# Fused attention and Fourier mixing on one core: full-form score tiles leave the visits, and the first batch's tables, turns and norm are rearranged

## The chip, the cores and the metric

The kernel runs on one core of a Trainium2 chip. TensorE (PE in the views, its weight loads PEld) multiplies matrices into PSUM, VectorE (DVE), ScalarE (ACT) and GpSimd (POOL) do the rest, and SyncE (SP) and GpSimd issue transfers. The metric is the device time of one execution in microseconds, lower is better.

## What is computed

```
scores = q @ k.T / sqrt(64);  attn = max(scores, 0)**2 / 448;  a = attn @ v     # 8 batches, 12 heads, 448 x 64
x = a as (8, 448, 768)
u = x + real(fft2(x over rows and columns))
un = (u - mean(u)) / sqrt(var(u) + 1e-6)          # over the 768 columns
out = u + max(un @ w_ch1, 0) @ w_ch2              # 768 -> 3072 -> 768
```

The inputs and the output are float32 in memory. The matmuls take bf16 operands and sum in float32.

## The kernel before

**Tiling.** Scores are made transposed, keys on the partitions. A batch has 12 heads in three groups of four. A group's keys are cut into seven tiles for the score stage: tiles 0 to 2 and 4 to 6 belong to a pair of heads each, one head on partitions 0 to 63 and one on 64 to 127, and their two matmuls of 64 rows run side by side (array form 64*128 in the trace, *row form* below). Tile 3 holds the last 64 keys of two heads at a time, zero-padded to 128 rows, and its two matmuls use the whole array (128*128, *full form*; `r == 3` in `score`, L993 to L1004). ScalarE takes a tile from PSUM with a relu (L1017, `squares`), VectorE or ScalarE squares it (L1034 or L1031, `square`), and `value` (L865) multiplies it with v: the full-form tile in one matmul (L870), the others in pairs of 64 columns each (L875, 128*64, *column form*). Six such value sets make a batch's attention. Then `fold` scales it into xT (L721 and L719 for the first batch).

**Mixing.** The transforms are matmuls with cosine and sine tables: over the channels (`first_channels`, L1457, for the first batch; L1482 after), a copy to bf16 (`pc`, L1501), over the rows (L1079, L1294). A mean and variance by BN_STATS, a square root on ScalarE, a norm into un, and a turn of un by matmuls (`turn`, L1180) give unT, which the first projection (L1986) reads. The later batches are stored and turned by transfers.

**Tables.** `build_dft` forms angles in turns on VectorE (L372 to L376: multiply and round to an integer, subtract it, take the absolute value) and sines on ScalarE (L381). `seq_table` forms the row tables on GpSimd (L406 to L414), VectorE (L421 to L425) and ScalarE (L431). `root_table` loads the square-root functions on ScalarE (L448).

**What sets the order.** Every stage is a generator that asks for its next operation; `ORDER`, a string of codes (L74), says for each step which of the waiting generators goes on. `CHOICES` (L109) fixes their decisions by number. So the order of every engine is written out, and a kernel's own rules count only where neither string nor table decides. From the second batch on, attention runs in *visits* between the projection matmuls: `attention` (L882) puts out up to three score tiles and one value set in one step, `LEAD` (L2220) says how far ahead of the projections. Three PSUM buffers of two banks (psS, pool BS) hold score tiles, two single banks (psF, BF) values and projections. Until the first channel matmuls, `warming` (L2202) fills TensorE with matmuls whose result is not used (L2216); `turn` has some too (L1178, L1185).

**The first batch.** `load_group` (L504) issues loads on GpSimd; for its first group the indices of the tables and the identity follow the load of k. `turn_on_pe` (L654) turns q and k by transposes (L671) and a copy (L678). `first_tail` (L1057) runs rows, norm and turns of the first batch; the last 64 rows of its second tile, which belong to the second group of columns, are turned by a matmul of their own (`turn_rows`, L1255) and copied (L1260). In the prediction, the *first projection* is the first matmul of L1986.

## Time and profile before

| | |
|---|---|
| median of 3 timed runs | 564.68 us (564.63 to 565.0) |
| the profiled execution | 564.12 us |
| its span, first to last instruction | 562.1 us |
| TensorE's mean granted clock | 0.999 |
| moved by DMA | 82.46 MB, mean 147 GB/s |
| HBM | 62.91 MB read, 26.25 MB written |

The span leaves out what the execution does before the first and after the last instruction, some 2 us. A row of the timeline has the start in us from the span's start, the length in us, the engine, the line, the operation, output and inputs by name with their shapes, and a count of instructions; behind it in brackets the idle time before it and what ended that. Lengths of matmuls overlap, so their spacing is read from their starts. In the view of windows each pair is the busy time of an engine and its instructions.

### The profile page before, as it was taken

How to read it: one execution, taken by the hardware profiler on the slowest of the kernel's cores; microseconds unless marked ns; L12 is line 12 of the kernel's file. 1: busy time of each engine (PE TensorE's matmuls, PEld its weight loads, DVE VectorE, ACT ScalarE, POOL GpSimd, SP SyncE). 2: the span in 40 equal slices, each digit the busy share in tenths (PEclk: the TensorE clock that was granted, in tenths of full speed). 3: DMA queues.
4: the chain of work that ended last, by engine and by line, in shares of the span. 5: the costliest groups of instructions: out<-in, count | busy, mean ns of one | idle time of the engine just before them, and what ended most of it. 6: DMA issues, size and time to landing. Idle time of an engine off the chain costs nothing.

```text
span 562.1 us, 11345 instructions
## 1 busy us (share of the span) xinstructions
PE 555.1 (99%) x4306; PEld 363.7 (65%) x4306; DVE 427.1 (76%) x1035; ACT 330.2 (59%) x557; POOL 166.8 (30%) x255
## 2 busy tenths in 40 slices
...
GB/s 111 180 206 266 204 208 147 183 172 172 147 120 222 146 195 144 142 239 184 124 153 183 214 165 166 207 139 64 114 117 159 162 30 47 96 42 141 1 43 114
DMA packets 152692, 82.46 MB, mean 147 GB/s; under 512 B 118077, under 2 KB 147901, under 8 KB 152637
## 3 DMA queue, kind: packets, MB, share of 16 engines
...
q8 instruction: 34, 0.56, 0.4%
q14 instruction: 22, 0.17, 0.1%
HBM read 62.91 MB, written 26.25 MB: 159 GB/s over the span
## 4 chain that ended last, share of the span: by engine, by line
PE 95%; DVE 1%; DMA 1%; ACT 1%; issue 0%; POOL 0%; DVEq 0%; POOLq 0%
PE psF L1986 27%; PE psF L2126 22%; PE psS L1002 8%; PE psS L2126 7%; PE psS L1817 7%; PE psF L875 5%; PE psF L2015 4%; PE psS L1482 2%; PE psF L1817 2%; PE psF L2040 1%; PE psF L870 1%; DMA kn<-in_k_dram 1%; PE psS L875 1%; PE psF L671 1%; PE psS L1457 1%; PE psS L1290 1%
## 5 line engine op out<-in xcount | busy, mean ns | idle before, releaser
L1017 ACT ACTIVATE sq<-psS 128x896 bf16<-128x896 f32 x168 | 145.9, 918 | 39.5 <-PE psS L1002 39.2
L1986 PE MATMUL psF<-unT,w 128*128 128x256 bf16 (+1 forms) x1296 | 165.6, 285 | 0.0
L1986 PEld LDWEIGHTS <-w 128*128 128x128 bf16 x1296 | 124.9, 98 | 38.0 <-issue 5.8
L2126 PEld LDWEIGHTS <-hT 128*128 128x128 bf16 x720 | 69.8, 98 | 47.0 <-issue 2.1
L1034 DVE TENSOR_TENSOR sq<-sq 128x896 bf16<-128x896 bf16 x138 | 82.5, 620 | 10.5 <-ACT sq L1017 9.9
L1973 ACT ACTIVATE hT<-psF 128x512 bf16<-128x512 f32 (+3 forms) x132 | 63.6, 503 | 41.3 <-PE psF L1986 40.8
L2126 PE MATMUL psF<-w,hT 128*128 128x384 bf16 x336 | 59.4, 326 | 0.0
L1674 DVE TENSOR_TENSOR o<-psF,o 128x384 f32<-128x384 f32 x73 | 40.4, 553 | 22.2 <-PE psF L2126 16.7
L1002 PE MATMUL psS<-qkT 64*128 64x448 bf16 (+1 forms) x336 | 51.8, 355 | 1.0 <-DVE qkT L678 0.9
L1832 ACT COPY copies<-psS 128x256 f32<-128x256 f32 x51 | 17.7, 376 | 53.5 <-PE psS L1817 40.2
L1391 POOL DMA_INDIRECT ubot<-u,backs x15 | 16.0, 1064 | 75.9 <-DVE u L1327 46.7
L1002 PEld LDWEIGHTS <-qkT 64*128 64x128 bf16 (+1 forms) x336 | 12.9, 94 | 32.7 <-issue 26.9
L524 POOL DMA_DIRECT2D qn<-in_q_dram x21 | 15.4, 735 | 61.7 <-DVE qkr L631 47.2
L875 PE MATMUL psF<-sq,vn 128*64 128x448 bf16 x234 | 31.5, 363 | 0.0
L1817 PEld LDWEIGHTS <-w 128*128 128x128 bf16 x288 | 28.2, 98 | 4.4 <-issue 0.7
L1334 DVE BATCH_NORM_STATS2 stats<-u 112x6 f32<-112x384 f32 (+2 forms) x56 | 29.8, 550 | 1.5 <-POOL u L1325 1.3
L737 DVE TENSOR_SCALAR xT<-psF 128x224 bf16<-128x224 f32 x56 | 19.8, 386 | 14.4 <-PE psF L875 14.1
L1391 POOL DMA_INDIRECT nbot<-un,backs x12 | 14.3, 1190 | 52.9 <-ACT un L1353 51.7
L1353 ACT ACTIVATE un<-u,small 112x768 bf16<-112x768 f32 (+2 forms) x28 | 28.7, 1029 | 1.3 <-DVE small L1340 0.9
L524 POOL DMA_DIRECT2D kn<-in_k_dram x21 | 16.1, 768 | 44.8 <-DVE qkr L631 37.8
L499 POOL DMA_DIRECT2D kn<-in_k_dram x42 | 25.8, 623 | 9.8 <-PE psF L1986 7.9
L1031 ACT ACTIVATE sq<-sq 128x896 bf16<-128x896 bf16 x30 | 28.3, 950 | 0.4
...
## 6 DMA issues: line engine op xcount, KB each, us to landing
...
```

What stands on the lines that cost most here:

```text
L524: nc.gpsimd.dma_start(out=to, in_=src[b, hs, 0:rows].rearrange("h (p j) d -> p h (j d)", j=j))
L875: nc.tensor.matmul(av[h * Dh:(h + 1) * Dh, 0:S], lhsT=vn_home[:, at:at + Dh], rhs=sq[:, h, :], start=start, stop=stop, skip_group_check=True)
L1002: nc.tensor.matmul(sc[:, h, 0:S].rearrange("k (c q) -> k c q", c=4), lhsT=flat[ps, k0:k0 + KB], rhs=qT[ps, pair], start=True, stop=True)
L1017: nc.scalar.activation(r, sc[:, :, 0:S], AF.Relu)
L1034: nc.vector.tensor_tensor(r, r, r, op=ALU.mult)
L1334: nc.vector.bn_stats(stats[:n, hf, :], u[:n, hf * (D // 2):(hf + 1) * (D // 2)])
L1391: nc.gpsimd.indirect_dma_start(out=bot, out_offset=bass.IndirectOffsetOnAxis(ap=(back if b < PAR else back2)[ch][:n], axis=0), in_=get(us[ ...
L1674: nc.vector.tensor_tensor(o[:, cols], pc[:, cols], o[:, cols], op=ALU.add)
L1817: nc.tensor.matmul(ps[:, 0:N], lhsT=lhs, rhs=rhs[:, m], start=(start and m == 0), stop=(stop and m == 2), skip_group_check=True)
L1973: nc.scalar.activation(hs, ps, AF.Relu)
L1986: nc.tensor.matmul(ph[:, i * N:(i + 1) * N], lhsT=w1_sb[m][hf][:, (jj + i) * 128:(jj + i + 1) * 128], rhs=unT[:, m, 0:N], start=(m == 0), ...
L2126: nc.tensor.matmul(pc[:, cols], lhsT=lhs[i], rhs=rhs[i][:, cols], start=(start and i == 0), stop=(i == KP - 1), skip_group_check=True)
```

## The change

- **Visits** (`attention`): outside the early visits, a full-form tile that is next gets a step of its own with no values. Otherwise a visit takes the tiles up to the next full-form one, that is one set of three. Where the values use a score buffer because two chains of the second projection are open, the visit takes no scores instead of up to two. LEAD falls from 2.9 to 2.5.
- **Tables**: the absolute value is an AND on the bits. The row tables are formed on VectorE alone from the channel tables' column indices, right after those; GpSimd's four steps and a rounding step on VectorE go. The table of square roots no longer waits for a copy.
- **First loads and turns**: the indices come right after the load of q. The first group's k is turned in two parts: three quarters as soon as the main part of k is there, the last quarter (filled by two later loads) by four transposes and one copy.
- **First norm and turn**: the third tile's norm goes from one GpSimd operation to two halves on ScalarE. The second tile is turned by 127 columns at once, and the later 64 are copied from the same bank (`second_part`), which then is held until this copy; the extra six matmuls go.
- **Squares**: the first batch's last square is no longer tied to ScalarE.
- **Order**: ORDER and CHOICES are new. In the whole program ScalarE has 14 squares instead of 30, VectorE 154 instead of 138. VectorE also takes some more of the projection's relus.

Of the two tables one line each; the rest of the difference in full, without context:

```diff
-CODES = '0123456789ABCDEFGHIJKLMNOPQRSTUVWXYZ'
+CODES = '0123456789ABCDEFGHIJKLMNOPQRSTUVWXY'
...
-    '009000000200999999999999999991111N1N029919999909199G102NN10991F111888MM4400F11L88L88884L088M84L1',
+    '000900000200999919999919919991N1N999102199G19NN10029912G902NN299225522G1M99M99919005M199N95M1099',
...
-    78: 0, 80: 1, 94: True, 99: False, 177: False, 190: True, 209: True, 226: 2, 238: True,
+    94: True, 107: 1, 121: False, 142: 4, 152: 2, 191: False, 232: True, 239: True, 252: 0,
...
@@ -363,0 +365,2 @@
+    SEQ_AT, SEQ_RANK = 3, 0.3
@@ -376 +379,2 @@
-            nc.vector.scalar_tensor_tensor(g, f, -1.0, f, op0=ALU.mult, op1=ALU.max)
+            nc.vector.tensor_scalar(g.bitcast(mybir.dt.int32), f.bitcast(mybir.dt.int32), 0x7FFFFFFF, None,
+                                    op0=ALU.bitwise_and)
@@ -384,0 +389 @@
+        nc.vector.tensor_scalar(row[:, 0:2], row[:, 4:6], 1.0 / S, None, op0=ALU.mult)
@@ -398,0 +404,2 @@
+            if m == SEQ_AT:
+                yield from seq_table()
@@ -399,0 +407,2 @@
+        if SEQ_AT == 3:
+            yield from seq_table()
@@ -403,9 +412,3 @@
-        f = work.tile([128, 4 * KH], FP32, name="dfty", tag="uA", bufs=1)
-        g = work.tile([128, 4 * KH], FP32, name="dfty", tag="uB", bufs=1)
-        yield need("POOL", 0.55)
-        nc.gpsimd.iota(drow[:, 0:2], pattern=[[128, 2]], base=0, channel_multiplier=1,
-                       allow_small_or_imprecise_dtypes=True)
-        nc.gpsimd.iota(dcol[:, 0:SX], pattern=[[1, SX]], base=0, channel_multiplier=0,
-                       allow_small_or_imprecise_dtypes=True)
-        yield need("POOL", 0.3)
-        nc.gpsimd.tensor_scalar(drow[:, 0:2], drow[:, 0:2], 1.0 / S, None, op0=ALU.mult)
+        f, g = (work.tile([128, 4 * KH], FP32, name="dfty", tag=t, bufs=1)[:, 0:2 * SX] for t in ("uA", "uB"))
+        whole = g.bitcast(mybir.dt.int32)
+        cols = dcol2.rearrange("p (t k) -> p k t", t=2)[:, 0:SX // 2]
@@ -413,4 +416,9 @@
-            e = yield need("POOL", 0.45)
-            nc.gpsimd.tensor_scalar(f[:, i * SX:(i + 1) * SX], dcol[:, 0:SX], drow[:, i:i + 1], None, op0=ALU.mult)
-        f, g = f[:, 0:2 * SX], g[:, 0:2 * SX]
-        sch.add(seq_sines(f, g, e + LATENCY["POOL"]), (0, 0.3))
+            at = slice(i * SX, (i + 1) * SX)
+            fi, wi = (y[:, at].rearrange("p (k t) -> p k t", t=2) for y in (f, whole))
+            yield need("DVE", dve(SX))
+            nc.vector.tensor_scalar(wi, cols, drow[:, i:i + 1], None, op0=ALU.mult)
+            yield need("DVE", dve(SX))
+            nc.vector.scalar_tensor_tensor(fi, cols, drow[:, i:i + 1], wi, op0=ALU.mult, op1=ALU.subtract)
+        e = yield need("DVE", 0.4)
+        nc.vector.tensor_scalar(whole, f.bitcast(mybir.dt.int32), 0x7FFFFFFF, None, op0=ALU.bitwise_and)
+        sch.add(seq_sines(f, g, e), (0, SEQ_RANK))
@@ -420,7 +427,0 @@
-        e = yield need("DVE", 0.4, [e])
-        nc.vector.tensor_scalar(g.bitcast(mybir.dt.int32), f, 1.0, None, op0=ALU.mult)
-        yield need("DVE", 0.55)
-        nc.vector.tensor_tensor(f, f, g.bitcast(mybir.dt.int32), op=ALU.subtract)
-        e = yield need("DVE", 0.4)
-        nc.vector.tensor_scalar(g.bitcast(mybir.dt.int32), f.bitcast(mybir.dt.int32), 0x7FFFFFFF, None,
-                                op0=ALU.bitwise_and)
@@ -446,2 +447,2 @@
-        yield need("SP", 0.0, [dft_ready, last_relu, first_copied])
-        yield need("ACT", 1.5, [first_copied])
+        yield need("SP", 0.0, [dft_ready, last_relu])
+        yield need("ACT", 1.5, [dft_ready])
@@ -480 +481 @@
-    arrived = {}
+    arrived, main_keys, ends_turned = {}, Cell(), Cell()
@@ -484,0 +486,2 @@
+        if (i, x) == (0, 1) and len(arrived[i, x]) == 1:
+            main_keys.t = landed[-1]
@@ -528 +531 @@
-            if i == 0 and x == 1:
+            if i == 0 and x == 0:
@@ -531,0 +535 @@
+            if i == 0 and x == 1:
@@ -587 +590,0 @@
-        yield from seq_table()
@@ -660 +663,3 @@
-        turned[b][g] = (pairs[:, :, 4 * KB:].rearrange("q r (c p) -> q r c p", c=4), flat, (KB, 4 * (KB + R)))
+        first = i == 0
+        turned[b][g] = (pairs[:, :, 0:4 * R].rearrange("q r (c p) -> q r c p", c=4), flat[:, 4 * R:], (KB, 4 * (KB + R)))
+        w = 4 * R + (3 if first else 4) * KB
@@ -663 +668 @@
-                e1 = yield need("PE", 4 * 0.07, ready[i][x:x + 1], [] if x else [BF],
+                e1 = yield need("PE", 4 * 0.07, [main_keys] if first and x else ready[i][x:x + 1], [] if x else [BF],
@@ -668,2 +673,2 @@
-                n, at = ((R, 4 * KB), (KB, 0))[x]
-                for c in range(4):
+                n, at = ((R, 0), (KB, 4 * R))[x]
+                for c in range(3 if first and x else 4):
@@ -678 +683 @@
-            copy(pairs[:, r], pt[:, 0:4 * (KB + R)])
+            copy(pairs[:, r, 0:w], pt[:, 0:w])
@@ -680,0 +686,12 @@
+        if first:
+            e1 = yield need("PE", 4 * 0.07, ready[i][1:2], [BF])
+            ptf = BF.take()
+            pt = ptf.bitcast(BF16)[:, 0:2 * KB].rearrange("q (r p) -> q r p", r=2)
+            for r in range(2):
+                for h in range(2):
+                    nc.tensor.transpose(pt[h * Dh:(h + 1) * Dh, r], loads[i][1][:, 3, 2 * r + h, :], ident)
+            e2 = yield need("DVE", 0.28, [e1 + LATENCY["PE"]])
+            nc.vector.tensor_copy(pairs[:, :, w:], pt)
+            BF.give(ptf, e2)
+            ends_turned.t = e2 + LATENCY["DVE"]
@@ -863 +880,3 @@
-        return turned_at[b][g] if r == 3 else [turned_at[b][g][r > 3]]
+        if r == 3:
+            return turned_at[b][g] + [ends_turned] * (b == 0 and g == 0)
+        return [turned_at[b][g][r > 3]]
@@ -895 +914,13 @@
-            n = min(1 if few else 3, NB - p)
+            if not few and p < NB and p % 7 == 3 and left is None and p + 1 - past(pv) <= room:
+                lead = b + p / NB
+                lead -= LEAD - SLOPE * (B - lead)
+                own = lambda: progress[0] >= lead
+                e = yield need("PE", 2 * mm(S), turned_for(b, p), [BS], own)
+                sc = score(b, p)
+                p += 1
+                fresh.append(p)
+                sqs[p - 1] = [None, Cell(), None]
+                sch.add(squares(b, [(p - 1, sc, e)], sqs), (0.2, 0.2))
+                continue
+            n = min(1 if few else 3, NB - p, NB if few else (3 - p) % 7 or 7)
@@ -915 +946 @@
-                        homes, n = BS, min(n, 2)
+                        homes, n = BS, 0
@@ -1021 +1052 @@
-            sch.add(square(b, r, e + LATENCY["ACT"], sqs[i][1], b == 0 and i == NB - 1), (0.2, 0.2))
+            sch.add(square(b, r, e + LATENCY["ACT"], sqs[i][1]), (0.2, 0.2))
@@ -1028,2 +1059,2 @@
-    def square(b, r, t, done, scalar):
-        if scalar or b >= ELASTIC[0] and sooner(t, "ACT", act(2 * S), "DVE", dve2(2 * S)):
+    def square(b, r, t, done):
+        if b >= ELASTIC[0] and sooner(t, "ACT", act(2 * S), "DVE", dve2(2 * S)):
@@ -1171,0 +1203,2 @@
+            if t == 1:
+                idn, w = rev[:, 0:127], 127
@@ -1182,0 +1216,2 @@
+            if t == 1:
+                BUN[0].free.append(e)
@@ -1198 +1233,2 @@
-                BS.give(pts[t][0], last)
+                if t != 1:
+                    BS.give(pts[t][0], last)
@@ -1204,0 +1241,8 @@
+        def second_part():
+            e = yield need("DVE", dve(6 * 64), [done[1][0]])
+            nc.vector.tensor_copy(groups[1][2][:, :, 0:64].rearrange("p (h m) w -> p h m w", h=2),
+                                  pts[1][0][:, :, 0:384].rearrange("p h (m w) -> p h m w", w=128)[:, :, :, 63:127])
+            BS.give(pts[1][0], e)
+            second_un[0].t = e + LATENCY["DVE"]
@@ -1224 +1268,2 @@
-        yield from norm(2, 0, "POOL")
+        yield from norm(2, 0, "ACT")
+        yield from norm(2, 1, "ACT")
@@ -1244 +1289 @@
-        sch.add(turn_rows(uns[0][1], max(t_un[1]), 128, rev[:, 63:127], 0, 64, "DVE", second_un[0]), (1, 1))
+        sch.add(second_part(), (1, 1))
@@ -1257,2 +1301,0 @@
-        if done is second_un[0]:
-            BUN[0].free.append(e)
@@ -2220 +2263 @@
-    LEAD, MIXED, SPARE, ELASTIC = 2.9, 1, 0.5, (1, 99)
+    LEAD, MIXED, SPARE, ELASTIC = 2.5, 1, 0.5, (1, 99)
```

**Three places in the order.** Rows have the line, the operation, output and inputs, and the output's shape; line numbers are those of each kernel.

TensorE, second batch, in the early projections; psS_1169 and psS_1172 are row-form tiles (their second and both matmuls), psS_1175 is the full-form tile, qkT the turned q and k. Before:

```order
L1002 LDWEIGHTS qkT_919
L1002 MATMUL psS_1169<-qkT_919 128x448
L1002 LDWEIGHTS qkT_919
L1002 MATMUL psS_1172<-qkT_919 128x448
L1002 LDWEIGHTS qkT_919
L1002 MATMUL psS_1172<-qkT_919 128x448
L1002 LDWEIGHTS qkT_919
L1002 MATMUL psS_1175<-qkT_919 128x448
L1002 LDWEIGHTS qkT_919
L1002 MATMUL psS_1175<-qkT_919 128x448
L1986 LDWEIGHTS w1_0_0_432
L1986 MATMUL psF_1183<-unT_682,w1_0_0_432 128x384
```

After, where the full-form tile of the same group stands (psS_1144):

```order
L2029 LDWEIGHTS w1_5_0_516
L2029 MATMUL psF_1135<-unT_685,w1_5_0_516 128x384
L1033 LDWEIGHTS qkT_910
L1033 MATMUL psS_1144<-qkT_910 128x448
L1033 LDWEIGHTS qkT_910
L1033 MATMUL psS_1144<-qkT_910 128x448
L2029 LDWEIGHTS w1_0_0_444
L2029 MATMUL psF_1148<-unT_685,w1_0_0_444 128x384
```

The full-form tile has left the two row-form ones and stands alone between two groups of projection matmuls; the next three row-form tiles follow a value set further on.

ScalarE, first batch, from the last relus (sq<-psS) to the first row copies (u). Before:

```order
L1017 ACTIVATE sq<-psS 128x896 x2
L719 ACTIVATE xT_111<-psF 128x224 x2
L1031 ACTIVATE sq<-sq 128x896
L719 ACTIVATE xT_111<-psF 128x224 x2
L431 ACTIVATE seqm<-dfty,few 128x480 x2
L431 ACTIVATE nseq<-dfty,few 128x480
L1501 CAST pc<-psS 128x2x193 x2
L678 COPY qkT<-psF 128x960
L448 ACT_TABLE_LOAD
L448 ACTIVATE drow<-few 128x1
L1131 COPY u<-psS 128x384
L1115 ACTIVATE small<-small,few 128x1
```

After:

```order
L736 ACTIVATE xT_111<-psF 128x224 x2
L1048 ACTIVATE sq<-psS 128x896
L432 ACTIVATE seqm<-dfty,few 128x480 x2
L432 ACTIVATE nseq<-dfty,few 128x480
L736 ACTIVATE xT_111<-psF 128x224 x2
L449 ACT_TABLE_LOAD
L449 ACTIVATE drow<-few 128x1
L1544 CAST pc<-psS 128x2x193 x2
L683 COPY qkT<-psF 128x960
L1162 COPY u<-psS 128x384
L1146 ACTIVATE small<-small,few 128x1
```

The square (L1031) is gone, the sines (L431, now L432) stand ahead of the last copy into xT, and the table load ahead of the pc copies instead of among the row copies.

VectorE, from the end of the memsets to the first copies of turned q and k. Before:

```order
L385 TENSOR_SCALAR drow<-drow 128x3
L372 TENSOR_SCALAR dftr<-dcol_114,drow 128x386
L374 SCALAR_TENSOR_TENSOR dfty<-dcol_114,drow,dftr 128x386
L376 SCALAR_TENSOR_TENSOR dfty<-dfty 128x386
L372 TENSOR_SCALAR dftr<-dcol_114,drow 128x386
L374 SCALAR_TENSOR_TENSOR dfty<-dcol_114,drow,dftr 128x386
L376 SCALAR_TENSOR_TENSOR dfty<-dfty 128x386
L441 TENSOR_SCALAR channeg<-chan_117 128x386
L372 TENSOR_SCALAR dftr<-dcol_114,drow 128x386
L374 SCALAR_TENSOR_TENSOR early<-dcol_114,drow,dftr 128x386
L376 SCALAR_TENSOR_TENSOR early<-early 128x386
L441 TENSOR_SCALAR channeg<-chan_118 128x386
```

The next row there is the first copy (L678). After, from the third table on:

```order
L375 TENSOR_SCALAR dftr<-dcol_114,drow 128x386
L377 SCALAR_TENSOR_TENSOR early<-dcol_114,drow,dftr 128x386
L379 TENSOR_SCALAR early<-early 128x386
L683 COPY qkT<-psF 128x832
L442 TENSOR_SCALAR channeg<-chan_118 128x386
L683 COPY qkT<-psF 128x832
L695 COPY qkT<-psF 128x2x128
L442 TENSOR_SCALAR channeg<-chan_119 128x386
L419 TENSOR_SCALAR dfty<-dcol_114,drow 128x240
L421 SCALAR_TENSOR_TENSOR dfty<-dcol_114,drow,dfty 128x240
L1065 TENSOR_TENSOR sq<-sq 128x896
```

The first copy stands one negation earlier, the last operation of a table is a TENSOR_SCALAR, and the row tables (L419, L421) stand between the first squares.

60 lines of the change are left out of this document (30 added, 30 removed), and 37 rows, old and new, of the table CHOICES.

## The prediction

> **What bounds the kernel now.** I read the page first: busy shares and the chain of work that ended last.
>
> ```profile
> span 562.1 us, 11345 instructions
> PE 555.1 (99%) x4306; PEld 363.7 (65%) x4306; DVE 427.1 (76%) x1035; ACT 330.2 (59%) x557; POOL 166.8 (30%) x255
> PE 95%; DVE 1%; DMA 1%; ACT 1%; issue 0%; POOL 0%; DVEq 0%; POOLq 0%
> ```
>
> TensorE is busy for 99% of the span, and 95% of the chain is TensorE. After the start, then, the time is the number of matmuls times their spacing, plus what the spacing loses between matmuls of unlike shape. The order of the program shows 4306 matmuls before and 4302 after, so columns streamed hardly change. What can change is the lost spacing, the waits, and the start, where a busy TensorE proves little because the page counts warming matmuls (L2216) as work.
>
> The view of waits, TensorE alone, from 60 us to the end, has one row:
>
> ```profile
> PE psF L1817 <- DVE hT L1837: 0.3, 1, 0.3
> ```
>
> Nearly no wait is left to remove after 60 us. There are two places to look: the form changes inside a visit, and the first 48 us.
>
> **Term 1: form changes.** The timeline of TensorE around one visit; columns are start, length, line, operands, array form, count:
>
> ```profile
> 49.52 0.55 PE L1002 MATMUL psS<-qkT 128*128 128x448 bf16 x2
> 49.91 3.10 PE L1986 MATMUL psF<-unT,w 128*128 128x384 bf16 x18
> 52.85 0.35 PE L870 MATMUL psF<-sq,vn 128*128 128x448 bf16 x1
> 53.13 0.76 PE L875 MATMUL psF<-sq,vn 128*64 128x448 bf16 x6
> 53.82 0.74 PE L1002 MATMUL psS<-qkT 64*128 64x448 bf16 x6
> 54.49 2.12 PE L1986 MATMUL psF<-unT,w 128*128 128x384 bf16 x12
> ```
>
> Read starts, since lengths of matmuls overlap. Two full-form score matmuls take 49.52 to 49.91, 0.19 us each, and the projection matmuls follow without a gap. Eighteen of those take 2.94 us, 0.163 each, and the full-form value matmul at 52.85 follows without a gap too. From 52.85 to 54.49 the visit takes 1.64 us. Its columns are one full matmul (0.19) and six pairs that run side by side (6 x 0.19), 1.33 us, plus some 0.03 between the pairs of L875. The other 0.28 us go to three changes of form: full to 64 columns, to 64 rows, back to full. That is **0.094 us a change**; a full-form tile between projection matmuls changes nothing.
>
> I counted the visits from the first projection matmul on in both orders. Before: 40 visits with values and row-form scores (3 changes each), 14 with row-form scores alone (2), 2 with values alone (2). After: 32, 9 and 10, and 20 full-form tiles alone, 19 of them with no change. With single changes at joins the orders have 154 and 136 in the visits; the second group of transposes keeps its 4. So 18 fewer: 18 x 0.094 = **-1.7 us**. The gain is less than a set of three full visits would suggest, because eight more value visits now stand without scores and pay two changes each; that is in the count. All of it is on the path, since TensorE is the chain there. A lone tile waits for one score bank, where a set waited for up to three, and only projections queue behind it. The lead of 2.5 instead of 2.9 lets attention run later; that costs nothing unless TensorE comes to wait, and stands in the bounds of the waits.
>
> The Trainium skill, page "TensorE: Matmul & The Clock Gate", section "Single matmul latency", gives a warm matmul whose drain is not hidden a constant of 398 cycles at 2.4 GHz beside its columns; as an estimate from that page a form change would cost 0.166 us, eighteen 3.0 us, and the time would be 560.5. The rows above show little more than half of that, and the rows decide.
>
> **Term 2: the first 48 us.** Nothing below rests on TensorE's busy time. It follows the chain from the tables on VectorE through the ScalarE relus to the first projection matmul.
>
> ```profile
> 3.08 0.18 POOL L310 IOTA drow<- 128x3 f32 x1
> 3.30 0.59 DVE L385 TENSOR_SCALAR drow<-drow 128x3 f32<-128x3 f32 x1 [0.98 <-POOL drow L310]
> 4.00 0.44 DVE L372 TENSOR_SCALAR dftr<-dcol,drow 128x386 int32<-128x386 f32 x1
> 5.12 0.56 DVE L376 SCALAR_TENSOR_TENSOR dfty<-dfty 128x386 f32<-128x386 f32 x1
> 9.31 0.65 DVE L678 COPY qkT<-psF 128x960 bf16<-128x960 bf16 x1
> 30.30 0.41 DVE L425 TENSOR_SCALAR dfty<-dfty 128x480 int32<-128x480 int32 x1
> 2.18 0.82 POOL L524 DMA_DIRECT2D qk<-in_k_dram  x1
> 6.82 0.48 PE L671 MATMUL psF<-ident,qk 128*64 128x128 bf16 x7
> 10.43 15.93 ACT L1017 ACTIVATE sq<-psS 128x896 bf16<-128x896 f32 x19
> ```
>
> *To the first relu.* The iotas pass the load of k (0.82 us of GpSimd), so L385's place starts at about 2.48; one more tiny operation stands there (0.2, an estimate from the 0.18 of small ones here), and the first table starts at 3.4 instead of 4.00, -0.6. Each table ends in a tensor_scalar on integers instead of L376. L425 is the same operation on 480 elements in 0.41; for 386 I take 0.36, -0.2 on each of three tables. Its bounds are 0.2 (columns alone at L425's rate) and 0.56 (no gain). One negation instead of two ahead of the first copy, -0.17. The copy of 9.31 moves to about 7.9. The load of k starts some 0.6 us later; its transposes began at 6.82 with time to spare, and at worst start at 7.45, which puts the copy at 8.2. Then four extra transposes wait for that copy's bank, about 0.3. The first relu starts at about 9.25 instead of 10.43.
>
> *To the last value.* The relus are 15.93 / 19 = 0.84 apart, and with two pairs of copies between them the last one ends at 27.9. VectorE is slower than that:
>
> ```profile
> 15.55 0.69 DVE L721 TENSOR_SCALAR xT<-psF 128x224 bf16<-128x224 f32 x2
> 16.68 0.65 DVE L678 COPY qkT<-psF 128x960 bf16<-128x960 bf16 x1
> 23.93 3.48 DVE L1034 TENSOR_TENSOR sq<-sq 128x896 bf16<-128x896 bf16 x6
> 30.63 0.83 DVE L796 TENSOR_TENSOR fold<-xT 128x225 bf16<-128x225 bf16 x4
> 30.75 0.38 PE L875 MATMUL psF<-sq,vn 128*64 128x448 bf16 x2
> ```
>
> It has 21 squares at 0.57 (the last was ScalarE's), four copies at 0.57 and three pairs of L721 at 0.6 (from start to next start), eight folds at 0.2 and five new sequence-table operations. Those run on 240 strided elements, which no row shows; the nearest are L372 (0.44) and L374 (0.62) on 386. I take 0.35 and 0.45, with 0.41 for the last, 2.0 in all; the bounds are 1.2 and 2.5. Together 19.6 us from 9.5, so the last square ends at 29.1 and its values run at 29.15 instead of 30.75.
>
> *To the rows.*
>
> ```profile
> 31.18 0.61 ACT L719 ACTIVATE xT<-psF 128x224 bf16<-128x224 f32 x2 [1.38 <-PE psF L875]
> 31.67 1.28 ACT L431 ACTIVATE seqm<-dfty,few 128x480 bf16<-128x480 f32 x2
> 29.66 1.16 PE L1457 MATMUL psS<-chan,fold 128*128 128x386 bf16 x6
> 31.43 0.70 PE L2216 MATMUL psS<-warm 128*128 128x252 bf16 x5
> 31.97 0.25 PE L1457 MATMUL psS<-chan,fold 128*128 128x193 bf16 x1
> 34.06 0.39 PE L671 MATMUL psF<-ident,qn 112*64 112x112 bf16 x8
> 34.61 0.54 PE L1079 MATMUL psS<-pc,seqm 128*128 128x384 bf16 x2
> ```
>
> Before, 24 channel matmuls stood behind the warming ones, 0.087 us each (31.97 to 34.06). After, behind the last value pair (0.3) stand 2 wide ones (0.36), 12 narrow (1.04), 11 warming (1.19) and 8 narrow (0.70): 3.6 us, ending at 32.75, -1.3. The three sines (0.64 each) come ahead of the last copy and end at 29.8, the copy (0.61) at 30.4, the last fold at 30.9, the square-root table (1.28, row below, and 0.3 for its first use) at 32.0: all beside the warming matmuls, which set the time. Rows start at 33.3.
>
> *To the first projection.*
>
> ```profile
> 35.68 1.28 ACT L448 ACT_TABLE_LOAD   x1
> 37.69 0.49 PE L1079 MATMUL psS<-pc,seqm 128*128 128x384 bf16 x2 [0.25 <-ACT u L1131]
> 42.87 0.29 ACT L1115 ACTIVATE small<-small,few 112x1 f32<-112x1 f32 x1 [0.99 <-DVE small L1109]
> 43.75 0.67 ACT L1154 ACTIVATE un<-psF,small 112x384 bf16<-112x384 f32 x1
> 46.84 0.95 ACT L678 COPY qkT<-psF 128x960 bf16<-128x960 bf16 x1
> 47.91 1.14 PE L1986 MATMUL psF<-unT,w 128*128 128x384 bf16 x6
> ```
>
> The wait of 0.25 for a bank goes, because the table load no longer stands among the copies. Against that, the third norm moves from GpSimd (L1152) to ScalarE in two halves of 0.67, ahead of the last root. That root waits until about 43.25 on the old clock instead of 42.87, and behind it are the last scale, norm, turn and copies: **+0.4**. The six matmuls of the extra turn go, but the first projection waited for the copy at 46.84 and not for TensorE, so I count nothing. The sum is -1.3 - 0.25 + 0.4 = **-1.15 us**; the projection starts near 46.75.
>
> GpSimd loses 4 us of sequence table, yet its later weight loads wait for earlier ones to land, so the loads come no sooner:
>
> ```profile
> 35.88 0.54 POOL L563 DMA_DIRECT2D w<-in_moe_w_ch_dram  x1 [1.28 <-DMA kn<-in_k_dram]
> ```
>
> The first norm on GpSimd stands behind this load and one of v, ends near 38.2, and its turn needs it at 40.4.
>
> **The sum.** -1.7 - 1.15 = -2.85. The profiled execution took 564.12 us (span 562.1); 561.3 after the change. The median of the timed runs is 564.68, 0.56 above it; on that scale I predict **561.8 us**. Ends: the start between -0.5 (tables no faster, new operations at 2.5) and -2.2 (VectorE keeps pace with the relus, the norm costs nothing); waits after 48 us between -0.7 and +1.5, since the order behind the start is new throughout.
>
> **Rivals.**
> 1. *The start is given back to a load.* The chain shows the third group's k for the second batch:
>
> ```profile
> 49.49 7.46 DMA kn<-in_k_dram
> ```
>
> It released TensorE near 57 us. If it lands no earlier, a projection that starts 1.15 us earlier waits 1.15 us longer there: 564.7 - 1.7 = 563.0. Against it: the new GpSimd order issues this load ahead of an indirect store. Chance 0.17.
>
> 2. *VectorE becomes the bound (slower).* ScalarE squares fall from 30 to 14, so VectorE gains 16 x 0.62, about 10 us, and some relus.
>
> ```profile
> 250.00:300.00 50.00, 50.00 (x383) 31.65 (x382) 42.95 (x101) 33.51 (x48) 17.92 (x24) 1.00 0.95 158
> ```
>
> In this 50 us stretch (busy time: PE, PEld, DVE, ACT, POOL) VectorE has 42.95, 86%; the added work, spread over 350 us, makes it about 89%. A late square then holds a value visit. There are 42; 2.85 us are lost from 0.07 us at each, and 0.15 us at each gives 561.8 + 6.3 = 568.1. Against it: the waits row above, next to nothing at 86%. Chance 0.06 slower, and 0.08 that half of it cancels the gain (564.5).
>
> 3. *Form changes dearer than 0.094 in the visits that go.* With a drain as long as a whole full-form matmul, 0.19, eighteen are worth 3.4 us: 560.1. All three in the visit above speak against it; 0.03.
>
> 4. *Order and tables move work, but TensorE hides it anyway.* Then only TensorE's own 1.7 counts, and a start pinned by the loads gives 563, as in rival 1.
>
> My forecast keeps 0.66. Faster by more than 0.2% (below 563.55; about what a measurement of this kernel can tell from no change) holds the forecast, rivals 1 and 3 but for their edge: 0.81. Within: 0.12. Slower: 0.07. The range 560.2 to 564.0 takes both ends of the start and most of the waits; 0.1 lies above, 0.1 below.
>
> **What would show it.** First relu near 9.3, last value near 29.2, rows near 33.3, first projection near 46.8; TensorE from there to the end 1.7 us shorter; a lone full-form tile that costs 0.38 us and no gap. Wrong if ScalarE's root for the last tile starts more than 0.4 us late, if a wait for VectorE or for k appears on TensorE after 48 us, or if the eight value visits without scores show more than two changes each.

## The result, and the profile after

The change made the kernel slower: **571.3 us**, median of 4 runs (568.88 to 573.43), against 564.65 for the kernel before (564.24 to 565.0). The ratio is 1.0117 [1.0076, 1.0158]. Forecast were 561.8 us and faster. The ratios here and below compare fast runs alone; a run over 1.5% above the fastest of its kernel (one of a1, one of after_again) is left out of them, though it stands in the medians and ranges. The profiled execution took 571.37 us, 7.25 more than the one of before. The page after, in its head, its busy shares and the engines' shares of the chain:

```profile
span 569.6 us, 11349 instructions
PE 554.6 (97%) x4302; PEld 365.1 (64%) x4302; DVE 442.1 (78%) x1062; ACT 315.7 (55%) x536; POOL 165.2 (29%) x249
PE 86%; DMA 8%; DVE 2%; POOL 2%; ACT 1%; issue 1%; DVEq 0%; POOLq 0%
```

The chain of before was 95% TensorE with 1% of DMA. Now 8% is DMA: somewhere the kernel waits for a transfer. The waits of TensorE: three rows of the start (to 50 us), then all rows from 50 to 115 us, and all from there to the end; behind the colon stand the sum, the count and the longest:

```profile
PE psF L676 <- DMA qk<-in_k_dram: 1.2, 1, 1.2
PE psF L693 <- DMA qk<-in_k_dram: 0.7, 1, 0.7
PE psS L1213 <- ACT unT L1231: 0.6, 1, 0.6
...
PE psF L2058 <- DMA w<-in_moe_w_ch_dram: 2.7, 1, 2.7
PE psS L1033 <- DMA qkT<-qkr: 1.5, 1, 1.5
PE psF L889 <- DMA vn<-in_v_dram: 1.0, 1, 1.0
...
PE psF L889 <- DVE o L1717: 1.1, 1, 1.1
PE psS L1033 <- ACT sq L1048: 0.4, 1, 0.4
PE psS L1033 <- ACT xT L751: 0.2, 1, 0.2
```

The same view of before had one row after 60 us, 0.3 us. The largest wait now is for a piece of the second projection's weights. The chain around it, in order of time (start, length, what):

```profile
59.92 34.21 DMA w<-in_moe_w_ch_dram
94.13 0.04 issue
94.17 3.54 PE psF L2058 x12
```

The piece, issued before 59.92, lands at 94.13. TensorE's timeline ahead of that, after and then before:

```profile
91.06 0.41 PE L1525 MATMUL psS<-chan,diff 128*97 128x193 bf16 x3
94.17 3.54 PE L2058 MATMUL psF<-w,hT 128*128 128x384 bf16 x12 [2.70 <-DMA w<-in_moe_w_ch_dram]
```

```profile
89.07 0.41 PE L1482 MATMUL psS<-chan,diff 128*97 128x193 bf16 x3
89.32 2.11 PE L2015 MATMUL psF<-w,hT 128*128 128x384 bf16 x12
```

Two things are to be seen. The matmuls start 2.86 us late (91.30, where the matmuls ahead have streamed, to 94.17), and the same twelve take 3.54 us instead of 2.11. The windows view tells why; its last three columns are the granted clock, the DMA share and GB/s:

```profile
91.00:94.00 3.00, 0.47 (x6) 0.33 (x5) 0.00 (x0) 1.53 (x2) 0.00 (x0) 0.95 1.50 160
94.00:98.00 4.00, 3.83 (x15) 1.92 (x15) 0.89 (x2) 0.00 (x0) 2.53 (x4) 0.61 1.53 160
98.00:102.00 4.00, 4.00 (x27) 2.52 (x25) 2.40 (x6) 0.99 (x2) 4.00 (x7) 1.00 1.34 159
```

After the idle stretch TensorE ran about 3 us at half clock (0.61 over the 4 us), which costs some 1.4 us more. The profiled execution's time then splits by starts on TensorE:

| | before | after | difference |
|---|---|---|---|
| first projection matmul starts | 47.91 | 49.01 | +1.10 |
| single waits over 0.15 us behind it, slowed matmuls included | 1.14 | 9.23 | +8.09 |
| the rest, up to the last matmul | 509.45 | 507.71 | -1.74 |
| last matmul starts | 558.49 | 565.94 | +7.45 |

A wait here is what a spacing of two matmuls has beyond the columns of the first, and beyond 0.1 us where the array form changes. So TensorE's own work shrank as forecast, and waits ate that gain more than four times over. The spread of this kernel's runs goes in part with the slowed stretch: those above 571 us have a mean clock of 0.994 to 0.997, the one at 568.88 has 1.000.

### The profile page after: what moved, and what is told of

Its sections match the earlier page's. It is cut to its first block, busy times and chain, and to the rows that moved or that the text cites. A ratio compares the mean times of both kernels' runs of the same rounds, so it can differ in the third digit from the quotient of the medians.

```text
span 569.6 us, 11349 instructions
## 1 busy us (share of the span) xinstructions
PE 554.6 (97%) x4302; PEld 365.1 (64%) x4302; DVE 442.1 (78%) x1062; ACT 315.7 (55%) x536; POOL 165.2 (29%) x249
## 4 chain that ended last, share of the span: by engine, by line
PE 86%; DMA 8%; DVE 2%; POOL 2%; ACT 1%; issue 1%; DVEq 0%; POOLq 0%
PE psF L2029 24%; PE psF L2169 23%; PE psS L1860 8%; PE psS L1033 7%; DMA w<-in_moe_w_ch_dram 6%; PE psS L2169 5%; PE psF L894 4%; PE psF L2058 2%; PE psF L1860 2%; PE psS L1525 2%; DMA qkT<-qkr 2%; PE psF L2083 1%; PE psS L894 1%; PE psF L889 1%; PE psF L676 1%; DMA qk<-in_k_dram 1%
## 5 line engine op out<-in xcount | busy, mean ns | idle before, releaser
L1065 DVE TENSOR_TENSOR sq<-sq 128x896 bf16<-128x896 bf16 x154 | 91.9, 619 | 13.5 <-ACT sq L1048 12.9
L2016 ACT ACTIVATE hT<-psF 128x512 bf16<-128x512 f32 (+2 forms) x123 | 60.1, 506 | 35.4 <-PE psF L2029 33.8
L2169 PE MATMUL psF<-w,hT 128*128 128x384 bf16 x378 | 67.4, 326 | 0.0
L1717 DVE TENSOR_TENSOR o<-psF,o 128x384 f32<-128x384 f32 x78 | 43.0, 552 | 27.6 <-PE psF L2169 16.4
L1875 ACT COPY copies<-psS 128x256 f32<-128x256 f32 x57 | 20.0, 376 | 41.7 <-PE psS L1860 36.7
L1434 POOL DMA_INDIRECT ubot<-u,backs x15 | 18.5, 1236 | 59.2 <-DVE u L1370 50.4
L1434 POOL DMA_INDIRECT nbot<-un,backs x12 | 13.0, 1084 | 71.5 <-ACT un L1396 50.8
L1033 PEld LDWEIGHTS <-qkT 64*128 64x128 bf16 (+1 forms) x336 | 15.3, 94 | 26.1 <-issue 17.8
L754 DVE TENSOR_SCALAR xT<-psF 128x224 bf16<-128x224 f32 x60 | 21.2, 384 | 12.9 <-PE psF L894 12.6
L894 PE MATMUL psF<-sq,vn 128*64 128x448 bf16 x228 | 30.2, 362 | 0.0
L2058 PE MATMUL psF<-w,hT 128*128 128x384 bf16 x144 | 26.3, 338 | 2.7 <-DMA w<-in_moe_w_ch_dram 2.7
```

Source lines behind the costliest of these rows:

```text
L894: nc.tensor.matmul(av[h * Dh:(h + 1) * Dh, 0:S], lhsT=vn_home[:, at:at + Dh], rhs=sq[:, h, :], start=start, stop=stop, skip_group_check=True)
L1033: nc.tensor.matmul(sc[:, h, 0:S].rearrange("k (c q) -> k c q", c=4), lhsT=flat[ps, k0:k0 + KB], rhs=qT[ps, pair], start=True, stop=True)
L1065: nc.vector.tensor_tensor(r, r, r, op=ALU.mult)
L1434: nc.gpsimd.indirect_dma_start(out=bot, out_offset=bass.IndirectOffsetOnAxis(ap=(back if b < PAR else back2)[ch][:n], axis=0), in_=get(us[ ...
L1717: nc.vector.tensor_tensor(o[:, cols], pc[:, cols], o[:, cols], op=ALU.add)
L2016: nc.scalar.activation(hs, ps, AF.Relu)
```

## The experiments

Theory W: the weights are the cause. GpSimd issues them later, so the last piece of w2 lands after it is read, and a long wait also costs clock. Theory S: the start is the cause, above all the load of k behind the iotas. Each set of runs shared its runs of the kernel before (medians 564.40, 564.40, 564.45 and 564.50).

Why the weights are issued later stands in GpSimd's timeline, before and after:

```profile
19.22 0.19 POOL L341 TENSOR_TENSOR backv<-backv 128x1 f32<-128x1 f32 x1
20.05 0.42 POOL L348 TENSOR_SCALAR_AFFINE_SELECT order<-order 128x57 bf16<-128x57 bf16 x2
20.64 3.37 POOL L563 DMA_DIRECT2D w<-in_moe_w_ch_dram  x6
```

```profile
19.87 0.56 POOL L342 TENSOR_TENSOR backv<-backv 128x1 f32<-128x1 f32 x1
21.34 0.80 POOL L349 TENSOR_SCALAR_AFFINE_SELECT order<-order 128x57 bf16<-128x57 bf16 x2
22.66 3.32 POOL L567 DMA_DIRECT2D w<-in_moe_w_ch_dram  x6
```

The first weights leave at 22.66 instead of 20.64. The small index instructions ahead of them (`mirrors`) begin 0.53 us later and take 4.24 us instead of 2.75, though none of them changed: four of them take about two to three times as long (0.56 for 0.19 us, 0.46 for 0.18, 0.80 for 0.42, 0.60 for 0.24), the index tables and memsets no longer than before. Beside them VectorE runs two-input squares and copies without a pause. It isn't the change alone that does this: in the second run of the same kernel (after_again) three of the four took 0.20, 0.43 and 0.24 us and the weights left at 21.74, and in a run of before with a longer `mirrors` (b_late) the four took 0.41 to 1.31 us.

### Set 1: three edits of after, and all of them

**a1_tables**: `mirrors` moves behind the issue of the first six weight pieces.

```
-            if i == NG + 1 and x == 1 and 0 in parts:
-                yield need("POOL", 3.6)
-                mirrors()
...
         yield from load_w1(0)
+        yield need("POOL", 3.6)
+        mirrors()
```

> The changed kernel with one thing moved: GpSimd's twelve small table instructions (rev, backs, order) run behind the issues of the first six weight loads and not ahead of them. Nothing moves on the other engines. Theory W (the weights land late, and TensorE waits for what queues behind them): the first weight piece is issued near 18.5 us instead of 22.66 and lands near 25.4 instead of 27.33; the last piece of the second projection's weights lands near 92 instead of 94.13; the waits at 80.4 (1.1 us, a load of v) and at 91.2 (2.9 us) shrink to under 0.2 and under 1, with them the 1.4 us of slow matmuls behind the second; time 566 to 568 us. Rival V (the searched order asks too early, DMA order means little): the waits move by under 0.5 us in all and the time stays at 570 to 571.5. Rival S (the loss is made at the start, before the first projection): also 570 to 571.5, as the start is untouched.

Measured: 564.96 us (563.57 to 572.86, 10 runs), 1.0016 [0.9991, 1.0041]. The weights leave at 18.75, the last piece lands at 90.04, the wait for it is 0.9 us at a full clock, and the wait for v is gone. This one edit, which changes no computation, takes back nearly the whole loss, more than theory W forecast, though two of its ten runs still took over 570 us.

**a2_iota**: the iotas go back behind the first load of k (in `load_group`).

```
-            if i == 0 and x == 0:
+            if i == 0 and x == 1:
                 e = yield need("POOL", 0.55)
                 dft_indices()
```

> The changed kernel with one thing undone: the two index tables (iota) of GpSimd stand behind the issue of the first load of k again, as before the change, not ahead of it. Both theories: the main part of k lands near 6.3 us instead of 7.29, the first projection starts 1 to 1.6 us earlier than 49.01. Theory W: weights come only 0.5 us earlier, so TensorE reaches them 0.5 to 1 us sooner than they do and gives the gain back at the waits of 80 to 110 us: time 570.3 to 571.3. Rival S (what is gained at the start stays gained): 569.5 to 570.

Measured: 565.6 us (564.98 to 566.72, 7 runs), 1.0026 [1.0015, 1.0038]. Both theories missed: the last load of k lands at 7.51 as before, but the first relu starts at 10.25, since the copies behind the tables on VectorE are now late (a wait of 1.2), and the first projection starts only 0.3 us earlier. The gain stands at the weights instead: GpSimd reaches them at 21.16, the last piece lands at 90.97, and the wait is 1.2.

**a3_vfirst**: the loads of v of the third group go ahead of the first two pieces of w2.

```
         yield from load_group(NG + 2, (0, 1))
+        yield from load_group(NG + 2, (2,))
         yield from load_w2(range(2))
-        yield from load_group(NG + 2, (2,))
```

> The changed kernel with one thing moved: the three loads of v for the third group of the second batch are issued ahead of the first two 1.1 MB pieces of the second projection's weights, not behind them. Theory W, with contention: these loads have fallen together with a DMA transpose and two reloads of rows (they took 5.6 us of the queue from 76.06 to 81.61, before the change 1.6); ahead of the weights they take under 2 us, so the last weight piece lands near 90.5 us instead of 94.13, the waits at 80.4 and 91.2 us fall from 4.0 to under 1 and the slow matmuls go; time 566 to 568. If the 4 us of the queue are owed to the transposes whatever lies in it, the last piece lands after 93 and the time is 569.5 to 571 (only the wait at 80.4 goes). Rival V: 570 to 571.5.

Measured: 565.95 us (564.37 to 570.62, 10 runs), 1.0041 [1.0013, 1.0068]. The last piece still lands late (91.38, a wait of 1.2).

**a4_all**: all three edits.

> The three edits together (tables behind the first six weight loads, index tables behind the load of k, the three loads of v ahead of the second weights). Theory W: last weight piece near 88 us, no wait over 0.5 us for a load between 50 and 100 us, start 1 to 1.6 us earlier; what is left over the kernel before are the waits of 190 to 201 us (2.2) and some of the 1.6 us at 107: time 562.5 to 565. Rival V: at least 568, since the order asks too early whatever the loads do. Rival S: 569.5 to 570, the gain of the index tables alone.

Measured: 565.77 us (563.95 to 566.62, 7 runs), 1.0017 [1.0004, 1.003]. The last piece lands at 89.21 and nothing waits for it. In its place TensorE waits 1.3 us for transposed q and k (`qkT<-qkr`) at 103 us. It is no better than a1 alone, and above theory W's 562.5 to 565: a removed wait came back behind another transfer. Of theory S the table above leaves 1.10 us of the 7.45, the later first projection.

### Set 2: the same again, and other places

**after_again**: the changed kernel, unedited, for its spread.

> The changed kernel as it is, a second time, beside the others of this set: how far its time and the landing of its loads spread from run to run. The wait for the last weight piece was 2.9 us in the first profile, and the three edits of the set before, each of which brings that piece forward by some microseconds, gave 565.0, 565.6 and 566.0 with runs up to 572.9. Theory W (TensorE asks for the piece at about the moment it lands, so the time hangs on the transfers): median 569 to 572, the lowest and highest run over 3 us apart, the kernel before within 1 us. Against it: a spread as small as that of the kernel before.

Measured: 569.07 us (565.79 to 574.48, 7 runs), 1.0092 [1.0058, 1.0125]. The profiled run took 565.96: the last piece of w2 lands at 91.57, the wait is 1.1 and the clock stays full. The same instructions with the same order thus land this piece at 91.57 in one run and at 94.13 in another; the first weights left at 21.74 there and at 22.66 here. The spread over 3 us is what theory W forecast.

**b_late**: before, with the first pair of instructions of `mirrors` run ten times, to make its weights late.

```
+        for _ in range(10):
-        nc.gpsimd.memset(rev, 0.0)
+            nc.gpsimd.memset(rev, 0.0)
...
```

> The kernel before the change with one addition: two of GpSimd's table instructions (rev) run ten times and not once, so that the first weight load is issued about 5.7 us later; nothing else moves, and the searched order is that of before. Theory W: in the kernel before the last weight piece lands at 86.33 us and is read at 89.32, 3.0 us of slack; with the loads 5.7 us later it lands near 92, TensorE waits 2 to 3 us there and some of the matmuls behind run at half clock as in the changed kernel: 568 to 571 us. If the loss of the changed kernel comes from its order and not from late weights, the time stays within 1.5 us of 564.4.

Measured: 573.2 us (571.67 to 573.56, 4 runs), 1.0146 [1.0131, 1.0161]. It misses its aim: the sequence table behind it on GpSimd came late too, and the waits stand elsewhere.

```profile
PE psS L1458 <- DVE fold L797: 3.2, 1, 3.2
PE psF L871 <- DMA vn<-in_v_dram: 2.8, 1, 2.8
```

TensorE reaches the last piece of w2 only behind its landing at 93.79. The run says nothing on W. It says something on the clock: behind the wait of 2.8 us (at 61 us) the trace has 3.4 us at half clock, behind the longer one of 3.2 us (at 36 us) none.

**c1_sp**: after, with the reloads of rows ahead of the transposes of xn on SP. The end of that stretch in the order of SP:

```
-L861 DMA_TRANSPOSE xn<-xT_110 128x4x128
 L1688 DMA o<-utop_72 96x384
 L1688 DMA o<-ulow 32x384
-L861 DMA_TRANSPOSE xn<-xT_111 128x4x128
 L1688 DMA o<-ulow 65x384
 L1688 DMA o<-ubot_80 63x384
-L861 DMA_TRANSPOSE xn<-xT_111 128x4x128 x2
+L861 DMA_TRANSPOSE xn<-xT_110 128x4x128 x3
+L861 DMA_TRANSPOSE xn<-xT_111 128x4x128 x3
```

> The changed kernel with SyncE's queue alone changed: seven reloads of rows (four of them of 192 KB), which stand behind DMA transposes that wait for the values of the second batch, are issued ahead of the first of these transposes, as before the change. Before, 928 KB went over the other queue while the second weights were loaded (57.3 to 86.3 us), after, 1501 KB (58.5 to 94.1). Theory R (the reloads slow the weights because they fall into their time): the stretch from the first to the last of these weights shortens by 2 to 4 us, the last piece lands at 90 to 92 instead of 94.13, time 566 to 569. Rival (the 16 engines move the same bytes in any order, so a reload that goes earlier only pushes the weights back): the last piece lands within 1 us of where it did, 570 to 572.

Measured: 568.51 us (567.48 to 571.01, 4 runs), 1.0066 [1.0051, 1.008]. In the profiled run, the slowest, the last piece lands at 93.84, the wait is 3.1 and the half clock follows. The landing is the rival's, within 0.3 us of where it was, and the median is within 0.6 us of after_again.

**c2_dve**: a1, with VectorE's two additions into u ahead of three copies and relus, at one place only. It goes at the wait for `o` (1.1 us, third part of the waits). The stretch of after, VectorE and then GpSimd beside it:

```profile
187.50 0.55 DVE L1368 TENSOR_TENSOR u<-qs,xn 112x385 f32<-112x385 f32 x1
187.97 2.62 DVE L1370 TENSOR_TENSOR u<-tp,xn 112x383 f32<-112x383 f32 x1
190.52 0.54 DVE L1717 TENSOR_TENSOR o<-psF,o 128x384 f32<-128x384 f32 x1
...
188.45 0.93 POOL L1368 TENSOR_TENSOR u<-tp,xn 112x385 f32<-112x385 f32 x1
189.32 0.85 POOL L1370 TENSOR_TENSOR u<-qs,xn 112x383 f32<-112x383 f32 x1
```

The second addition takes 2.62 us where its neighbour takes 0.55, while GpSimd adds two operands too; `o` behind it, and so a bank of TensorE, is late. The edit, in the order of VectorE:

```
-L2144 TENSOR_TENSOR hT<-hT 128x256
-L633 COPY qkr<-qn 112x1024
-L2146 TENSOR_TENSOR hT<-hT 128x256
 L1367 TENSOR_TENSOR u<-qs,xn 112x385
 L1369 TENSOR_TENSOR u<-tp,xn 112x383
+L2144 TENSOR_TENSOR hT<-hT 128x256
+L633 COPY qkr<-qn 112x1024
+L2146 TENSOR_TENSOR hT<-hT 128x256
```

> The kernel a1_tables with one step of VectorE moved: its two additions for rows of the first-mix output (u), which ran beside GpSimd's two additions of the same kind, go ahead of two small additions and one copy (qkr), so that they are done before GpSimd begins. In the changed kernel, and in the three edits of the first set, the second of these additions took 2.63 us and not 0.55, and TensorE waited 1.26 us for the addition behind it and 0.9 us 10 us later. Theory P (the two engines shut each other out while both add): that instruction takes 0.6 us again, the waits at 183.7 and 194 us shrink by 1 to 2.2 us in sum: 563 to 564.2 us. Rival (VectorE is simply behind its work there, wherever the two additions stand): within 0.5 us of a1_tables, 564.5 to 565.5.

Measured: 563.45 us (562.58 to 570.06, 12 runs), 1.0003 [0.9978, 1.0027]. In its trace the additions stand clear of GpSimd's, which begin at 182.72:

```profile
180.10 0.55 DVE L1367 TENSOR_TENSOR u<-qs,xn 112x385 f32<-112x385 f32 x1
180.57 0.55 DVE L1369 TENSOR_TENSOR u<-tp,xn 112x383 f32<-112x383 f32 x1
```

The wait is gone. The time against before stays within the interval, so what shows this part is the trace. The collision itself has moved: at 183.41 another two-input instruction of VectorE (`hT`, 0.28 us elsewhere) takes 1.20 beside GpSimd's second addition, and TensorE doesn't wait for it. The Trainium skill, page "SBUF — State Buffer", section "Who interferes with whom", states that a VectorE instruction with two inputs in SBUF contends with a GpSimd instruction that reads SBUF, that the shared ports are an exclusive lock, and that the order of issue decides who blocks. The 2.62 against 0.55 agrees with the contention; VectorE's addition is stamped 0.48 us ahead of GpSimd's and was held all the same.

### Set 3: the deadline itself

**d2_more**: before, with three more loads of 384 KB ahead of w2, which the program throws away (the last piece is loaded again in its turn). This makes the weights late in an order that is otherwise that of before.

```
+            if i == 0:
+                w2_sb[3] = wpool.tile([128, 6, D], BF16, name="w2_3")
+                for j in range(3):
+                    nc.gpsimd.dma_start(
+                        out=w2_sb[3][:, 2 * j:2 * j + 2],
+                        in_=moe_w_ch2[2304 + j * 256:2560 + j * 256, :].rearrange("(j p) d -> p j d", p=128))
...
```

> The kernel before the change with one addition: ahead of the first piece of the second projection's weights, three loads of 384 KB are issued that write the last piece's data a first time (the last piece is loaded again in its turn, so the output is the same). Every other instruction and the order of all engines are those of before. By the pace of its loads (1.9 to 2.4 us for 384 KB) all that queues behind lands about 6 us later: the third group's v near 80 us instead of 74.05 (read at 79.02), the last weight piece near 92.5 instead of 86.33 (read at 89.32). Theory W: waits of about 1 us near 79 and 2 us near 90, matmuls at half clock behind them in some runs, a later third group: 568 to 570.5 us with a spread of over 2 us. Rival (late weights cost this order nothing, the loss of the changed kernel sits in its searched order): 564 to 565.5 and the small spread of before.

Measured: 569.49 us (567.86 to 571.32, 4 runs), 1.009 [1.0071, 1.011]. The last piece lands at 93.22 and the picture of after appears, wait and clock; waits from 60 us on, timeline, and windows:

```profile
PE psF L2021 <- DMA w<-in_moe_w_ch_dram: 2.9, 1, 2.9
PE psF L1823 <- DVE hT L1843: 0.3, 1, 0.3
```

```profile
93.27 3.29 PE L2021 MATMUL psF<-w,hT 128*128 128x384 bf16 x12 [2.93 <-DMA w<-in_moe_w_ch_dram]
```

```profile
94.00:98.00 4.00, 4.00 (x16) 2.10 (x15) 0.89 (x2) 0.26 (x1) 1.57 (x3) 0.57 1.57 178
```

The profiled run is 5.6 us longer than before's. The wait and the half clock are 4.5 of that; 1.05 lie ahead of the first projection, which the added loads, issued at 53.9, can't have caused. So late weights alone make most of 5 us out of a kernel that has none of the change's other parts. This is theory W, shown from the other side.

**d1_tx**: c2, with the third and fourth transposes of xn behind the fifth on SP, so that they do not share the queue with the last pieces.

```
-L860 DMA_TRANSPOSE xn<-xT_110 128x4x128
 L1687 DMA o<-utop_72 96x384
 L1687 DMA o<-ulow 32x384
-L860 DMA_TRANSPOSE xn<-xT_111 128x4x128
 L1687 DMA o<-ulow 65x384
 L1687 DMA o<-ubot_80 63x384
+L860 DMA_TRANSPOSE xn<-xT_111 128x4x128
+L860 DMA_TRANSPOSE xn<-xT_110 128x4x128
```

> The kernel c2_dve with SyncE's order changed in one place: the third and fourth DMA transpose of the second batch's values (xn) go behind the fifth, so that they start near 81 to 83 us and not at 66 and 72; before the change the third stood at 75.65 us. Theory T (each of these transposes takes some 1.6 us from the software queue while it runs, and two more of them than before fall into the load of the second weights): the stretch of the four weight pieces shortens by 2 to 3 us, the last piece lands near 88 us instead of 90.5, TensorE's wait of 1.1 us there goes and so do the disturbed runs: 562 to 562.7 us, no run over 565. Rival (as with the reloads, the order on the other queue changes nothing for the last piece): it lands at 90 to 91 and the time is that of c2_dve, 563 to 564 with runs up to 570.

Measured: 563.47 us (562.86 to 564.05, 11 runs), 0.9981 [0.9972, 0.9989]: faster than before. The last piece lands at 87.41 (c2: 90.50) and is read without a wait, earlier than theory T forecast, but the median is that of c2: what went is the spread, no run is over 565. A new wait stands behind the piece:

```profile
89.01 2.11 PE L2057 MATMUL psF<-w,hT 128*128 128x384 bf16 x12
102.50 0.74 PE L1032 MATMUL psS<-qkT 64*128 64x448 bf16 x6 [1.28 <-DMA qkT<-qkr]
```

**d3_vfirst**: c2 with the loads of v first, as in a3.

> The kernel c2_dve with the three loads of v for the second batch's third group ahead of the first two pieces of the second weights (the edit of a3_vfirst). With a3_vfirst the stretch of weights and v took 33.0 us and not 35.6, and with all three edits (a4_all) the last piece landed at 89.21 with no wait for it, but the wait at 101.6 us for a transpose (1.4 us) came in its place. Theory W: the last piece lands near 89, no wait there, part of the gain is given back at 101 us: 562.3 to 563.3, few runs over 565. Rival (the gain is given back whole): 563 to 564, as c2_dve.

Measured: 564.49 us (562.78 to 568.08, 12 runs), 1.0003 [0.9985, 1.0021]. No gain over c2; both theories forecast less time. Its profiled run waits 2.2 us for w2, which lands at 91.73, and the clock stays at 1.00 in every window behind it.

### Set 4: what is left

**e1_tx1**: c2, with only the fourth transpose behind the fifth.

```
-L860 DMA_TRANSPOSE xn<-xT_111 128x4x128
 L1687 DMA o<-ulow 65x384
 L1687 DMA o<-ubot_80 63x384
-L860 DMA_TRANSPOSE xn<-xT_111 128x4x128 x2
+L860 DMA_TRANSPOSE xn<-xT_111 128x4x128 x3
```

> The kernel c2_dve with one DMA transpose of the second batch's values (the fourth) behind the fifth; in d1_tx it was the third and the fourth. In d1_tx the last weight piece landed at 87.41 us and the wait for it went, but TensorE waited 1.35 us at 100.9 for a transpose of queries and keys that queued behind the ones put off. Theory T: with one put off, the last piece lands near 89, within 0.3 us of where it is read, and the wait at 100.9 shrinks under 0.6: 562.3 to 563.2 us. Rival (the engines of the transfers are full from 20 to 100 us, and each order only moves the wait from one place to the other): the two waits come to 1.2 to 1.5 us again, 563.2 to 563.8.

Measured: 563.92 us (562.58 to 567.35, 11 runs), 0.9994 [0.9981, 1.0007]. The last piece lands at 89.95 without a wait, and the wait for `qkT` stays (1.0 at 103 us): the wait moves between transfers rather than going.

**e2_norm**: e1, with the third norm of the first batch whole on GpSimd instead of in two halves on ScalarE.

```
-        yield from norm(2, 0, "ACT")
-        yield from norm(2, 1, "ACT")
+        yield from norm(2, 0, "POOL")
```

> The kernel e1_tx1 with the third norm of the first batch on GpSimd again, one instruction as before the change, and not in two halves on ScalarE. In the changed kernel TensorE loses 1.8 us between 40 and 50 us (0.62 and 0.76 of it before two turns that wait for ScalarE), before the change 1.0. Theory N (the norm's two halves on ScalarE hold up the copies that the turns wait for): the loss falls to 1.0 to 1.2, the first projection starts 0.6 to 0.8 us earlier than in e1_tx1 and the time falls by 0.5 to 0.8 if no transfer takes it back. Rival (the turns wait for other things, as the change also took one turn out and put a longer one in): the first projection moves by under 0.2 us.

Measured: **563.07 us** (562.0 to 563.19, 8 runs), 0.9972 [0.9961, 0.9982]: the best version, ahead of both kernels. From the rows' start to the first projection it takes 13.09 us, against 13.70 after and 13.30 before, the 0.6 us that theory N forecast. It still waits behind 50 us:

```profile
PE psS L1032 <- DMA qkT<-qkr: 1.3, 1, 1.3
PE psS L1032 <- ACT sq L1047: 0.4, 1, 0.4
PE psS L1032 <- ACT xT L750: 0.2, 1, 0.2
```

**b_iota**: before, with the iotas ahead of the load of k and nothing else.

```
-            if i == 0 and x == 1:
+            if i == 0 and x == 0:
                 e = yield need("POOL", 0.55)
                 dft_indices()
```

> The kernel before the change with one thing of it done: the two index tables (iota) of GpSimd ahead of the issue of the first load of k. The prediction's step: the tables of VectorE begin about 0.6 to 0.9 us earlier, the load of k stays off the path, the first relu comes at 9.5 to 9.8 us instead of 10.43 and the first projection as much earlier: 563.5 to 564. Theory K (the load of k is on the path as soon as it is issued later: in the five kernels with the index tables ahead its second half landed at 8.3 to 9.9 us, in the others at 7.5): the relu comes at 9.7 to 10.5 and what is gained goes where the third group's loads are waited for: 564.2 to 565.2, with a wider spread than that of before.

Measured: 564.64 us (564.35 to 565.66, 10 runs), 1.0006 [0.9997, 1.0015]. The last load of k lands at 8.65 instead of 7.55, TensorE waits 0.6 for it, and the first relu starts at 10.57 against 10.43. Moving the iotas alone gains nothing, as theory K said.

## Why the prediction was wrong

**The step that failed: "its later weight loads wait for earlier ones to land, so the loads come no sooner".** It asked whether the loads could come sooner and never whether they could come *later*. Nor did the sum hold the slack of any weight piece. It could be read from before, in the view of the tile w on GpSimd from 50 to 100 us:

```profile
L574 POOL DMA_DIRECT2D w<-in_moe_w_ch_dram x4: 823/844/852, 53.0 to 59.1; - x4
DMA to landing us min/median/max: 18.6/21.2/27.2
```

The last piece, issued at 59.13, lands 27.2 us later, at 86.33; it is read at 89.32 (timeline above). The slack was 2.99 us. After, it lands at 94.13, 7.8 later, and the landings on the way show where that comes from:

| lands at | before | after | a1_tables |
|---|---|---|---|
| first piece of w1 | 25.50 | 27.33 | 25.91 |
| last piece of w1 | 48.93 | 51.01 | 48.70 |
| first piece of w2 | 65.10 | 67.86 | 64.92 |
| last piece of w2 | 86.33 | 94.13 | 90.04 |

The later issue of the weights is carried on to the first piece of w2, 2.8 us. The other 5.0 us come between the first and the last piece of w2. Where the issue is put right (a1), 3.9 of these remain. So the larger part lies in that stretch, where the new order puts other transfers beside the weights, and the prediction held nothing for it either. What there does it is shown in part: d1, which takes two transposes out of the stretch, lands the piece 3.1 us earlier than c2. The bytes on the hardware queue don't tell: beside w2 it moves 928 KB before, 1501 after and 1155 in c1, where the piece still lands at 93.84. Neither part alone makes the loss: with a1's edit the wait falls to 0.9 us. A wait of 2.86 us was then dearer than itself, by the half clock.

**The bound of the waits, "between -0.7 and +1.5", failed with it**: measured +8.09. Of that, w2's wait and its slow matmuls are about 4.3 (2.86 + 1.4); `qkT` is 1.6, v 1.1, the wait for `o` 1.3, and two short ones near 201 us 0.9. "The order behind the start is new throughout" was the right reason; the size was not worked out from any slack.

**Term 1 was right**, in its mechanism too: -1.7 forecast, -1.74 measured, 0.097 us a change for eighteen. Counted matmul by matmul behind the first projection, the form changes 158 times before and 140 after, and a change takes 0.098 us beyond the columns before and 0.099 after. The lone full-form tile costs what was said, here from start to start 131.22 to 131.60, 0.38 us, without a gap:

```profile
131.22 0.54 PE L1033 MATMUL psS<-qkT 128*128 128x448 bf16 x2
131.60 1.58 PE L2029 MATMUL psF<-unT,w 128*128 128x256 bf16 x13
```

**Term 2, -1.15 forecast and +1.10 measured**, by its own steps:

| step | forecast | after | a1_tables |
|---|---|---|---|
| first relu starts | 9.25 | 10.53 | 9.44 |
| from there to the last values | 19.90 | 20.62 | 20.74 |
| from there to the rows | 4.15 | 4.16 | 4.17 |
| from there to the first projection | 13.45 | 13.70 | 13.70 |

*First relu.* The tables came sooner, as forecast: the first copy of turned q and k stands at 8.39 instead of 9.31. "At worst start at 7.45" held for the main load of k: its transposes start at 7.33. What failed is "four extra transposes wait for that copy's bank, about 0.3". Three of the four waited for the last load of k, which the sum did not hold: it lands at 9.85, 2.3 later than before.

```profile
8.39 0.57 DVE L683 COPY qkT<-psF 128x832 bf16<-128x832 bf16 x1
9.89 0.30 PE L693 MATMUL psF<-ident,qk 128*64 128x128 bf16 x3 [0.66 <-DMA qk<-in_k_dram]
10.53 1.73 ACT L1048 ACTIVATE sq<-psS 128x896 bf16<-128x896 f32 x2 [0.90 <-PE psS L1033]
```

With the iotas behind k (a2, a4) that load lands at 7.51 and 7.57. With the iotas first it lands at 8.24 to 8.39 in the six kernels that have `mirrors` behind the weights (a1, c2, d1, d3, e1, e2) and at 8.98 to 9.85 in those that don't (after twice, a3, c1); what links the two is not known. At 8.33 (a1) the relu came at 9.44, 0.19 off. In e1 it came at 10.74 although the load landed at 8.27, since TensorE ran at half clock from 7.73 to 11.14. So the mechanism held, and the wait for this load is worth up to 1.1 us (10.53 against 9.44).

*Last values.* VectorE's sum held: from the first relu to the end of the last square it takes 19.92 us (a1 20.05), 19.85 in the forecast. In it the five row-table operations took 2.7 us (a1 2.3) and not 2.0. Mis-sized was the step behind it. The forecast puts the last values 0.05 us behind the last square; they start 0.70 behind it (a1 0.69), because TensorE is at channel matmuls, without a gap, that stand ahead of them in its order:

```profile
29.83 0.62 DVE L1065 TENSOR_TENSOR sq<-sq 128x896 bf16<-128x896 bf16 x1
30.05 0.92 PE L1500 MATMUL psS<-chan,fold 128*128 128x386 bf16 x5
31.14 0.38 PE L894 MATMUL psF<-sq,vn 128*64 128x448 bf16 x2
```

*First projection.* The bank's wait was worth what was said: e2, where it is gone and the norm is back on GpSimd, is 0.21 shorter than before. The third norm on ScalarE cost 0.61 (13.70 against 13.09), not 0.4: the last root starts 0.31 later behind the rows than in e2 (8.27 against 7.96), about what was counted, and 0.30 more comes behind it, where ScalarE's copy of a turned tile waits 0.60 for TensorE instead of 0.21.

**The rivals.** Rival 1 (the start is given back to kn at 57 us) was not put to the test, as the start came later and not earlier; the same kind of loss came at other loads. Rival 2 (VectorE becomes the bound) did not come as it was put, since value visits do not wait for squares; but one wait for VectorE did, 1.1 us before 191.21, from a collision with GpSimd that no row of before showed; the prediction had named such a wait as a sign of being wrong. Rival 3 is refuted by -1.74 and by 0.099 us a change.

**What stays open.** Why the last load of k lands between 8.24 and 9.85 when it is issued a little later. Why w2 lands at 91.57 and at 94.13 with the same instructions; the earlier issue there accounts for 0.9 of these 2.6 us. Which of the transfers beside w2 hold it up, beyond d1's two transposes. What would end the wait of 1.0 to 1.3 us for `qkT` between 102 and 109 us (in a4, c1, d1, d3, e1 and e2, not in a1 or c2), and the 0.4 and 0.2 behind 192 us, wasn't tried. That the index instructions on GpSimd slowed because of VectorE's squares is argued from the timeline; no run took the squares away.
